# Attention and a gated feed-forward block on one core: stores of newly made weight parts stand four products later in the second pass

## The chip, the core and the metric

The kernel runs on one core of a Trainium2 chip. A core has several engines that run side by side, each through its own list of instructions in order: TensorE multiplies matrices (PE in the profile, its weight loads PEld), VectorE (DVE), ScalarE (ACT) and GpSimd (POOL) work element by element, and SyncE (SP) issues the transfers (DMAs) between the chip's large memory and the core's own memory. An engine that needs another's result waits for a semaphore, and everything behind the waiting instruction in its list waits too. The metric is the time of one execution in device microseconds; smaller is better.

## The reference: what is computed

Attention over 8 batches and 8 heads, 576 queries of 64 numbers each; keys and values are first averaged in groups of 8, so there are 72 of them. Its result, put together over the heads, is x, 4608 tokens of 512 numbers. A gated block follows:

```python
scores = scale * np.matmul(q, k_p.transpose(0, 1, 3, 2))   # k_p, v_p: means of 8
attn = softmax(scores)
x = (attn @ v_p) as 4608 x 512
gate = 1.0 / (1.0 + np.exp(-(x @ w_gate)))                 # w_gate: 512 x 1536
val = x @ w_val                                            # w_val:  512 x 1536
return (gate * val @ w_out)                                # w_out: 1536 x 512
```

## The kernel before

**Precision.** An operand of the feed-forward products is held as two parts, a high one and the rest, and a product is three matmuls (high by high, high by rest, rest by high). `split` (L165) makes the parts: a cast on ScalarE (L167), a subtraction on VectorE (L168).

**Seven products.** A 2 by 2 block product is made of seven smaller ones, m = 1 to 7 (`product`, L621 for its matmuls), instead of eight. For this the weights' quarters are added up: m = 1, 2, 3 take plain quarters of the weight, m = 4 to 7 sums of quarters. A product's result goes into a bank of TensorE's output memory; m = 1, 5 and 6 are copied out by ScalarE (L627, names sG1, sV5 and so on), m = 2, 3 and 7 are added to such a copy on VectorE (y, L633), then the gate side takes a sigmoid on ScalarE (L639) and the value side a multiplication by it on VectorE (h, L642). A bank can be filled again only when these have read it.

**Passes.** The tokens are cut in 12 blocks of 384, and a pass makes two of them: six passes. The weights of w_gate (G) and w_val (V) are cut in six pairs of columns, 0 to 5. In a pass, `hidden` goes through the pairs in the order `TURNS`, and for each pair through the 14 products of `SLOTS`, G and V mixed; then `second_sums` makes the second matmul (L834). Attention for the next pass's tokens runs as `tasks` between the products (scores L454, e L503, the exponential L508, attention times values L463).

**Weight parts.** Parts in use stand in a ring of eight buffers, `wpool`, tile name `parts`. The parts of a pair and kind are grouped as A (m = 1, 5), B (2, 6), C (3, 7) and D (4, 8; 8 is not used). A buffer holds one group, and after the group's last product it is loaded with the same group of the next pair (`loaded`, `reload`). In the text "G2C" is group C of gate pair 2.

**The second pass** is where the sums for pairs 0 to 4 are first made. The first pass has stored the plain parts (`kept...`) and the whole weights (`keptw...`) in the large memory. `prepare` loads a whole pair (512 KB, L254, tile w) and makes the four sums on VectorE (L255 to L257). `reload` with `fresh` then loads the group's plain part (256 KB, L297), splits the sum into the buffer's other half (L167, L168), and stores the new part (256 KB, `keep`, L213), so that later passes load both halves ready made. From the third pass on no part is made, but for pair 5, whose sums (`sums`, tile name sums) are made and stored early in the third pass.

**What sets the order.** The first pass is written out by hand (`ORDER`). From the second pass on a scheduler places each engine's instructions by times of its own, with the program's order as a start; an instruction passed to `tc.keep_in_program_order` keeps its place behind the last one before it on its engine. All transfers are issued on SP's one queue, in order: a store whose part isn't split yet holds every transfer behind it. SP also waits, at a transfer, for the one issued eight before.

Of the kernel before, what the change touches and what calls it, by code (L numbers as in the profile page):

```python
# [11 lines left out]
F32 = mybir.dt.float32  # L12
# [34 lines left out]
GROUPS = {"A": (1, 5), "B": (2, 6), "C": (3, 7), "D": (4, 8)}  # L47
# [77 lines left out]
def attention_then_ffn(ctx: ExitStack, tc: tile.TileContext, qT, kT, vm, vr, vn, sums8, wgv, wo, const, out, outT):  # L125
    nc = tc.nc
# [38 lines left out]
    def split(h, l, x):  # L165

        in_turn(nc.scalar.copy(h, x))  # L167
        in_turn(nc.vector.tensor_tensor(out=l, in0=x, in1=h.bitcast(F32), op=ALU.subtract))  # L168
# [3 lines left out]
    kept = {  # L172
        (kind, p, g): dram.tile([P, 2, 2 * HALF], F32R, name=f"kept{kind}{p}{g}")
        for p in range(NP) for kind in "GV" for g in GROUPS
    }
# [31 lines left out]
    def place(m):  # L207
        g = next(g for g, ms in GROUPS.items() if m in ms)
        return g, GROUPS[g].index(m)

    def keep(kind, p, m, t):
        g, i = place(m)
        nc.sync.dma_start(kept[kind, p, g][:, i].bitcast(F32), t.rearrange("p h n -> p (h n)").bitcast(F32))  # L213
# [52 lines left out]
    def sums(kind, p):  # L266

        if (kind, p) not in summing:
            fetch_for_sums(kind, p)
        w = summing.pop((kind, p))  # L270
        s = opool.tile([P, 4, HALF], F32, name="s4", tag="oparts")
        in_turn(nc.vector.tensor_tensor(out=s[:, 0:2], in0=w[:, 1:3], in1=w[:, 0:2], op=ALU.subtract))
        nc.vector.tensor_tensor(out=s[:, 2], in0=w[:, 2], in1=s[:, 0], op=ALU.subtract)
        nc.vector.tensor_tensor(out=s[:, 3], in0=w[:, 3], in1=s[:, 2], op=ALU.subtract)
        for i, ms in enumerate(((5, 7), (6, 4))):
            t = opool.tile([P, 2, 2, HALF], F32R, name="sums", tag="oparts")
            split(t[:, :, 0], t[:, :, 1], s[:, 2 * i:2 * i + 2])
            for k, m in enumerate(ms):
                keep(kind, p, m, t[:, k])
# [5 lines left out]
    def prepare(kind, p):  # L285
        summed[kind, p] = add_up(kind, p)

    def reload(kind, p, g, fresh=False):

        t = wpool.tile([P, 2, 2, HALF], F32R, name="parts", tag="parts")  # L290
        n = sum(m != 8 for m in GROUPS[g])
        for i, m in enumerate(GROUPS[g][:n]):
            parts[kind, p, m] = t[:, i]
        i = n - 1
        k = i if fresh else n
        if k:
            nc.sync.dma_start(  # L297
                t[:, :k].rearrange("p m h n -> p m (h n)").bitcast(F32), kept[kind, p, g][:, :k].bitcast(F32)
            )
        if fresh:  # L300
            split(t[:, i, 0], t[:, i, 1], summed[kind, p][:, SUM[g]])
            keep(kind, p, GROUPS[g][i], t[:, i])

    raws_o = {}

# [306 lines left out]
    def product(kind, p, m, stays=False):  # L612

        b = {1: "A", 6: "A", 7: "A", 4: "A", 2: "B", 5: "C", 3: "C"}[m]
        if m in (1, 2, 5):
            bank[kind, b] = ps.tile([P, BT], F32, name="chain", tag=CHAIN["GV".index(kind) * 3 + "ABC".index(b)])
        t, w, x = bank[kind, b], parts[kind, p, m] if stays else parts.pop((kind, p, m)), xo[m]
        for c in range(NC // 2):
            a = slice(c * P, (c + 1) * P)
            for k, (h, y) in enumerate(((0, 0), (0, 1), (1, 0))):  # L620
                nc.tensor.matmul(  # L621
                    t, lhsT=w[:, h, a], rhs=x[:, y, c],
                    start=(m in (1, 2, 5) and c == 0 and k == 0), stop=(c == 1 and k == 2), skip_group_check=True,
                )
        if m in (1, 5, 6):
            s = snap.tile([P, BT], F32, name=f"s{kind}{m}")
            nc.scalar.copy(s, t)  # L627
            seen[kind, m] = s
            return
        q = {2: (0, 0), 3: (0, 1), 7: (1, 1), 4: (1, 0)}[m]  # L630
        if m != 4:
            y = two.tile([P, BT], F32, name="y", tag="y")
            nc.vector.tensor_tensor(out=y, in0=t, in1=seen[kind, {2: 1, 3: 6, 7: 5}[m]], op=ALU.add)  # L633
        else:
            y = t
        if kind == "G":
            if m in (2, 7):
                gates[q[0]] = snap.tile([P, 2, BT], F32, name=f"gate{q[0]}")
            nc.scalar.activation(gates[q[0]][:, q[1]], y, AF.Sigmoid)  # L639
        else:  # L640
            f = 2 * p + q[1]
            nc.vector.tensor_tensor(  # L642
                out=hb[f // 4][:, f % 4, q[0] * BT:(q[0] + 1) * BT], in0=y, in1=gates[q[0]][:, q[1]], op=ALU.mult
            )

    def new_h(*ks):
        for k in ks or range(3):
            hb[k] = hpool.tile([P, NF // 3, 2 * BT], F32, name="h", tag=f"h{k}")
# [58 lines left out]
    def hidden(last, tasks, n):  # L707
        if n > 1:
            new_h()
        left = {}  # L710
        pairs = TURNS[n]
        for p, pair in enumerate(pairs):
            for i, (kind, m) in enumerate(SLOTS):
                if n == 1 and i == 3 and p + 1 < EARLY:
                    prepare("V", pairs[p + 1])
                if n == 1 and i == 10 and p + 2 < EARLY:
                    prepare("G", pairs[p + 2])
                if m < 0:
                    if p == 0:
                        continue  # L720
                    at, m = p - 1, -m
                else:
                    at = p
                stays = at + 1 == len(pairs) and not last
                product(kind, pairs[at], m, stays)
                if at + 1 < len(pairs):
                    loaded(kind, pairs[at], m, left, pairs[at + 1], n == 1)
                if n == 1 and i in (1, 4, 7, 10, 13) or n > 1 and (i % 3 == 2 or p == 0):
                    next(tasks, None)
                if n == 1:  # L730
                    if (p, i) in ((2, 4), (4, 4)):
                        first_sums(qs[1][p // 4])
                    if (p, i) in ((4, 7), (4, 11)):
                        operand(1, qs[1][i == 11], 1)
                    continue
                if p in (2, 4) and i == 4:
                    first_sums(qs[n][p // 2 - 1])
                if (p, i) in ((4, 10), (5, 6)):
                    operand(1, qs[n][p - 4], n)
                if n == 2 and (p, i) in ((1, 1), (2, 1)):  # L740
                    sums(*left_over.pop(0))
        for _ in tasks:
            pass

    def loaded(kind, p, m, left, then, fresh):

        g, i = place(m)
        left[kind, p, g] = left.get((kind, p, g), 0) + 1
        if left[kind, p, g] == sum(m != 8 for m in GROUPS[g]):
            reload(kind, then, g, fresh)  # L750
# [17 lines left out]
    def first_sums(q):  # L768

        at = len(s1)  # L770
        if at == 0:
            s1[None] = big.tile([P, 2, 2, BT], F32, name="s1", tag="big")
            at = 1
        s1[q] = s1[None][:, at - 1] if at < 3 else snap.tile([P, 2, BT], F32, name="s1", tag="gate0")
        minus(s1[q], quarter(q, 1, 0), quarter(q, 1, 1), ALU.add)
        if at < 3:
            third_sums(q)
# [9 lines left out]
    def operand(m, q, n):  # L787

        if m == 6:
            minus(s1[q], s1[q], quarter(q, 0, 0))  # L790
        if m == 3:
            minus(s1[q], quarter(q, 0, 1), s1[q])
        if m == 7 and q == qs[n][2]:
            third_sums(q)
        x = s1[q] if m in (5, 6, 3) else quarter(q, *{1: (0, 0), 2: (0, 1), 7: (1, 0), 4: (1, 1)}[m])
        hs = big.tile([P, 2, 2, BT], F32R, name="hs", tag="big")
        nc.scalar.copy(hs[:, 0], x)  # L797
        nc.vector.tensor_tensor(out=hs[:, 1], in0=x, in1=hs[:, 0].bitcast(F32), op=ALU.subtract)  # L798
        halves[m, q] = hs
# [387 lines left out]
    for n in range(NB // 2):  # L1187
        last = 2 * n + 2 == NB
        tasks, later = ahead[n:n + 2]
        steady[0] = n > 1  # L1190
        if n == 0:
            continue
        if n == 1:
            hidden_second(tasks)
        else:
            hidden(last, tasks, n)
        if last:
            build = iter(())
        else:
            build = operands()  # L1200
        if n < 1:
            second(tasks, build)
        else:
            second_sums(n, last, build, later)
# [46 lines left out]
```

## Time and profile before

| | |
|---|---|
| median of 3 runs | 975.35 us (972.98 to 976.16) |
| profiled execution | 973.47 us, span 971.7 us, mean granted clock of TensorE 0.993 |
| PE busy | 939.0 us, 97% of the span |
| DVE / ACT / POOL busy | 706.8 (73%) / 557.5 (57%) / 47.5 (5%) us |
| SP's transfer queue | 242.26 MB, 75.1% of 16 engines' span |
| chain that ended last | PE 71%, DVE 15%, DMA 7%, ACT 4%, issue 2% |

The span is the time from the first to the last instruction; 1.8 us of the execution lie around it. The chain that ended last is the row of work, followed back from the last instruction, that had nothing to spare. With PE busy for 97%, the kernel's length is PE's work plus the few stretches in which PE had to wait.

### The profile page before, as it was taken

To read this page: it belongs to the slowest core of one execution; us is meant where nothing else is said; L and a number is where in the kernel's file an instruction comes from. 1 tells how busy PE (TensorE), PEld (TensorE's weight loads), DVE (VectorE), ACT (ScalarE), POOL (GpSimd) and SP (SyncE) were. 2 spreads that over 40 slices of the span, in tenths; PEclk is the share of its full clock that TensorE was granted. 3 is DMA by queue.
4 is the path that set the end of the run, shared out by engine and by line. 5 is a ranking of instruction groups with operands and counts; after the bars stand their busy time and mean duration, and the time that the engine had idled before them with its cause. 6 is when DMAs were issued, how large, how long until landed. Compare 5 with 4: busy or idle time off the path is not lost.

```text
span 971.7 us, 15360 instructions
## 1 busy us (share of the span) xinstructions
PE 939.0 (97%) x5400; PEld 907.2 (93%) x5400; DVE 706.8 (73%) x1231; ACT 557.5 (57%) x1142; POOL 47.5 (5%) x67
## 2 busy tenths in 40 slices
PE   5899999999998999999999999999999999999998
PEld 4689998889998999999999999989999999999998
DVE  7999998787888878767796566599366578244474
ACT  6898966554666656645664555556355555233342
POOL 1210000000000000000000000000000000000000
PEclk8899999999999999999999999999999999999999
DMA  9978987769877377997479878567876637877566
GB/s 317 343 264 311 315 305 219 257 229 352 296 269 245 131 241 247 351 362 247 129 230 277 264 239 275 177 184 255 271 257 221 211 120 227 283 247 251 163 205 228
DMA packets 109883, 243.22 MB, mean 250 GB/s; under 512 B 11376, under 2 KB 45936, under 8 KB 108272
## 3 DMA queue, kind: packets, MB, share of 16 engines
q1 hardware_dynamic: 109808, 242.26, 75.1%
q8 instruction: 43, 0.70, 0.3%
q14 instruction: 32, 0.26, 0.1%
HBM read 191.88 MB, written 50.33 MB: 249 GB/s over the span
## 4 chain that ended last, share of the span: by engine, by line
PE 71%; DVE 15%; DMA 7%; ACT 4%; issue 2%; SPq 0%; DVEq 0%; ACTq 0%
PE chain L621 38%; PE acc L834 18%; PE chain L661 5%; PE acc L1147 3%; PE sc L454 3%; PE av L463 2%; DVE s L766 2%; DVE hs L798 1%; DMA out<-o 1%; DMA raw<-in_wgv 1%; DVE raw L197 1%; DVE w L199 1%; PE tp L542 1%; DVE zs L975 1%; DMA parts<-keptG1A 1%
## 5 line engine op out<-in xcount | busy, mean ns | idle before, releaser
L621 PE MATMUL chain<-xo,parts 128*128 128x384 f32 x2436 | 457.5, 341 | 7.6 <-ACT sG L627 2.5
L621 PEld LDWEIGHTS chain<-xo,parts 128*128 128x128 f32 x2436 | 424.0, 188 | 12.1 <-ACT sG L627 3.7
L834 PE MATMUL acc<-hs,oparts 128*128 128x384 f32 x1260 | 229.2, 336 | 3.2 <-DVE hs L798 2.8
L834 PEld LDWEIGHTS acc<-hs,oparts 128*128 128x128 f32 x1260 | 218.2, 188 | 6.0 <-DVE hs L798 4.4
L633 DVE TENSOR_TENSOR y<-chain,sG 128x384 f32<-128x384 f32 x87 | 47.8, 552 | 79.1 <-ACT sG L627 27.6
L661 PE MATMUL chain<-xo,parts 128*128 128x384 f32 x504 | 93.7, 340 | 0.8 <-ACT xs L1086 0.8
L661 PEld LDWEIGHTS chain<-xo,parts 128*128 128x128 f32 x504 | 87.9, 188 | 2.6 <-ACT xs L1086 1.1
L627 ACT COPY sG<-chain 128x384 f32<-128x384 f32 x87 | 41.5, 477 | 55.5 <-PE chain L621 55.1
L633 DVE TENSOR_TENSOR y<-chain,sV 128x384 f32<-128x384 f32 x87 | 47.5, 550 | 35.1 <-PE chain L621 26.4
L798 DVE TENSOR_TENSOR hs<-h,hs 128x768 fp32r<-128x768 f32 x60 | 58.1, 973 | 17.1 <-ACT hs L797 17.1
L627 ACT COPY sV<-chain 128x384 f32<-128x384 f32 x87 | 41.3, 476 | 50.0 <-PE chain L621 45.5
L639 ACT ACTIVATE gate<-y 128x384 f32<-128x384 f32 x87 | 45.5, 525 | 41.2 <-DVE y L633 40.7
L797 ACT CAST hs<-h 128x768 fp32r<-128x768 f32 x60 | 49.9, 834 | 25.4 <-PE acc L834 25.1
L536 POOL TENSOR_TENSOR pm<-e,rz 128x384 f32<-128x384 f32 x32 | 29.2, 912 | 610.7 <-DVE rz L516 224.7
L797 ACT CAST hs<-s 128x768 fp32r<-128x768 f32 x45 | 37.0, 835 | 34.4 <-PE acc L834 22.7
L1147 PE MATMUL acc<-oparts,hs 128*128 128x512 f32 x216 | 51.7, 392 | 0.4 <-DVE hs L1137 0.4
L642 DVE TENSOR_TENSOR h<-y,gate 128x384 f32<-128x384 f32 x87 | 49.0, 567 | 1.8
L798 DVE TENSOR_TENSOR hs<-s,hs 128x768 fp32r<-128x768 f32 x45 | 42.5, 954 | 8.3 <-ACT hs L797 8.0
L1147 PEld LDWEIGHTS acc<-oparts,hs 128*128 128x128 f32 x216 | 40.2, 188 | 8.7 <-DVE hs L1137 0.8
L454 PE MATMUL sc<-kbd,raw 128*128 128x144 f32 (+1 forms) x280 | 47.6, 308 | 0.0
L454 PEld LDWEIGHTS sc<-kbd,raw 128*128 128x128 f32 (+1 forms) x280 | 38.3, 187 | 6.6 <-issue 4.0
L546 DVE TENSOR_TENSOR pl<-tp,ph 128x384 fp32r<-128x384 f32 x32 | 17.6, 551 | 26.7 <-ACT ph L545 26.7
(186 smaller groups left out, 1182.0 us busy)
## 6 DMA issues: line engine op xcount, KB each, us to landing
oparts<-keptS SPq DMA_DIRECT2D x60, 512.0 KB, 4.4
oparts<-keptO SPq DMA_DIRECT2D x90, 256.0 KB, 3.8
raw<-in_wgv SPq DMA_DIRECT2D x12, 1024.0 KB, 6.7
raw<-in_qT SPq DMA_DIRECT2D x42, 192.0 KB, 4.3
out<-o SPq DMA_DIRECT2D x40, 192.0 KB, 4.3
raw<-in_kT SPq DMA_DIRECT2D x26, 288.0 KB, 4.1
raw<-in_vm SPq DMA_DIRECT2D x28, 256.0 KB, 4.1
raw_o<-in_wo SPq DMA_DIRECT2D x12, 512.0 KB, 4.4
```

Source lines behind the costliest of these rows:

```text
L454: nc.tensor.matmul(sc[lo - i * P:hi - i * P, i], lhsT=q[:, lo:hi], rhs=kbd[slot(b, p)], start=True, stop=True)
L536: nc.gpsimd.tensor_tensor(out=pm, in0=e[:, n, :, :KM], in1=rz[:, n, :, None].broadcast_to([P, 2 * QT, KM]), op=ALU.mult)
L621: nc.tensor.matmul(t, lhsT=w[:, h, a], rhs=x[:, y, c], start=(m in (1, 2, 5) and c == 0 and k == 0), stop=(c == 1 and k == 2), skip_group_ ...
L627: nc.scalar.copy(s, t)
L633: nc.vector.tensor_tensor(out=y, in0=t, in1=seen[kind, {2: 1, 3: 6, 7: 5}[m]], op=ALU.add)
L639: nc.scalar.activation(gates[q[0]][:, q[1]], y, AF.Sigmoid)
L642: nc.vector.tensor_tensor(out=hb[f // 4][:, f % 4, q[0] * BT:(q[0] + 1) * BT], in0=y, in1=gates[q[0]][:, q[1]], op=ALU.mult)
L661: nc.tensor.matmul(t, lhsT=w[:, c // 2, h, a], rhs=x[:, y, c % 2], start=(c == 0 and k == 0), stop=(c == NC - 1 and k == 2),)
L797: nc.scalar.copy(hs[:, 0], x)
L798: nc.vector.tensor_tensor(out=hs[:, 1], in0=x, in1=hs[:, 0].bitcast(F32), op=ALU.subtract)
L834: nc.tensor.matmul(acc[name, c], lhsT=w[:, k, h, c * P:(c + 1) * P], rhs=hs[:, y, k], start=(m in (1, 2, 5) and i % 3 == 0 and k == 0 and ...
L1147: nc.tensor.matmul(acc[i], lhsT=hss[f][:, y, a], rhs=oparts[f][:, w], start=(f == 0 and k == 0), stop=(f == NF - 1 and k == 2),)
```

## The change

`reload` no longer issues the store of a new part. It puts it on a list, `due`, with a count of 4. `keep_due`, called after each product of `hidden`, takes one from each count and issues the stores whose count is used up; it is also called at the head of every `reload`, for stores of the same kind and group (an older pair's) alone, and at the end of the pass for all that are left. Each of these stores is passed to `keep_in_program_order`, so that it stays behind the SP instruction traced just before it. Nothing is computed otherwise, and the same transfers are made.

```diff
     def reload(kind, p, g, fresh=False):
 
+        keep_due(room=(kind, g))
         t = wpool.tile([P, 2, 2, HALF], F32R, name="parts", tag="parts")
...
         if fresh:
             split(t[:, i, 0], t[:, i, 1], summed[kind, p][:, SUM[g]])
-            keep(kind, p, GROUPS[g][i], t[:, i])
+            due.append([LATER, kind, p, GROUPS[g][i], t[:, i]])
+
+
+    LATER = 4
+    due = []
+
+    def keep_due(all=False, room=None):
+        for d in due:
+            d[0] -= room is None
+        for d in [d for d in due if all or d[0] <= 0 or (d[1], place(d[3])[0]) == room]:
+            due.remove(d)
+            _, kind, p, m, t = d
+            g, i = place(m)
+            tc.keep_in_program_order(
+                nc.sync.dma_start(kept[kind, p, g][:, i].bitcast(F32), t.rearrange("p h n -> p (h n)").bitcast(F32))
+            )
...
                 if at + 1 < len(pairs):
                     loaded(kind, pairs[at], m, left, pairs[at + 1], n == 1)
+                keep_due()
...
         for _ in tasks:
             pass
+        keep_due(True)
```

Since the scheduler places the other instructions around these stores, all engines but POOL get another order, from about 230 us to about 554 us of the trace before. Three places follow. Lines of the kernel after are 1 higher for `reload`'s load (L298), L317 for the moved store, and 16 higher from there on (L642 becomes L658).

First SP, the transfers around the parts of pair 2, before. The names are those above; a store is `kept... <- parts`, a load `parts <- kept...`, and w8 is a whole weight loaded for its sums.

```order
L297 DMA parts_3203<-keptG2B_143 128x512
L380 DMA raw_4208<-in_qT 128x384
L213 DMA keptV1D_141<-parts_3175 128x512
L254 DMA w8_3289<-keptwG3_180 128x1024
L213 DMA keptG2B_143<-parts_3203 128x512
L297 DMA parts_3241<-keptG2C_144 128x512
L213 DMA keptG2C_144<-parts_3241 128x512
L297 DMA parts_3273<-keptV2A_146 128x512
L213 DMA keptV2A_146<-parts_3273 128x512
L213 DMA keptG2D_145<-parts_3285 128x512
L297 DMA parts_3317<-keptV2B_147 128x512
L254 DMA w8_3408<-keptwV3_181 128x1024
```

The same place on SP after:

```order
L298 DMA parts_3201<-keptG2B_143 128x512
L317 DMA keptG2A_142<-parts_3152 128x512
L254 DMA w8_3287<-keptwG3_180 128x1024
L298 DMA parts_3240<-keptG2C_144 128x512
L317 DMA keptG2B_143<-parts_3201 128x512
L298 DMA parts_3272<-keptV2A_146 128x512
L317 DMA keptG2C_144<-parts_3240 128x512
L298 DMA parts_3315<-keptV2B_147 128x512
L317 DMA keptV2A_146<-parts_3272 128x512
L317 DMA keptG2D_145<-parts_3283 128x512
L254 DMA w8_3406<-keptwV3_181 128x1024
```

The load of G2C now stands ahead of the store of G2B, and the load of V2B ahead of the store of G2D; the load of the whole V3 still stands behind the store of G2D.

Next DVE, a little later, before: L255 is the first sum of the whole V3 and waits for its load.

```order
L642 TENSOR_TENSOR h_2381<-y_3337,gate1_3239 128x384
L255 TENSOR_TENSOR w8_3408<-w8_3408 128x512
L633 TENSOR_TENSOR y_3428<-chain_3421,sG1_3374 128x384
L256 TENSOR_TENSOR w8_3408<-w8_3408 128x256
L168 TENSOR_TENSOR parts_3385<-w8_3289,parts_3385 128x256
L418 TENSOR_TENSOR vl0_101<-vs_3125,vh0_96 64x64 x2
L257 TENSOR_TENSOR w8_3408<-w8_3408 128x256
L500 TENSOR_REDUCE m_3261<-sc_3257 128x6
L642 TENSOR_TENSOR h_2381<-chain_3246,gate1_3239 128x384
L503 TENSOR_TENSOR e_3208<-sc_3257,m_3261 128x432
```

The same place on DVE after:

```order
L519 TENSOR_TENSOR e_3206<-sc_3256,m_3260 128x432
L649 TENSOR_TENSOR y_3336<-chain_3244,sV5_3270 128x384
L649 TENSOR_TENSOR y_3426<-chain_3419,sG1_3372 128x384
L255 TENSOR_TENSOR w8_3406<-w8_3406 128x512
L168 TENSOR_TENSOR parts_3384<-w8_3287,parts_3384 128x256
L658 TENSOR_TENSOR h_2381<-y_3336,gate1_3238 128x384
L529 TENSOR_REDUCE zs_3207<-e_3206 128x12
L256 TENSOR_TENSOR w8_3406<-w8_3406 128x256
L413 TENSOR_REDUCE ks_4210<-raw_4211 128x72
L168 TENSOR_TENSOR parts_3402<-w8_3177,parts_3402 128x256
L649 TENSOR_TENSOR y_3451<-chain_3375,sG6_3417 128x384
L562 TENSOR_TENSOR pl_3120<-tp_3115,ph_3119 128x384
```

e and a y have moved ahead of L255. The last h of V1, which reads the chain's bank (chain_3246 before, chain_3244 after), stood eight rows behind L255 (the doubled row counts as two) and is eleven behind it now: three rows follow the last one shown, a small zs, L257 and then this h.

Last ACT, where the copy sG6 of G2 is made, before:

```order
L639 ACTIVATE gate0_3430<-y_3428 128x384
L167 CAST parts_3404<-w8_3179 128x256
L508 ACT_TABLE_LOAD
L508 ACTIVATE e_3208<-e_3208 128x864
L797 CAST hs_3688<-h_2383 128x768
L627 COPY sG6_3419<-chain_3367 128x384
```

The same place on ACT after:

```order
L524 ACT_TABLE_LOAD
L524 ACTIVATE e_3206<-e_3206 128x864
L643 COPY sV5_3492<-chain_3485 128x384
L655 ACT_TABLE_LOAD
L655 ACTIVATE gate0_3428<-y_3426 128x384
L167 CAST parts_3402<-w8_3177 128x256
L643 COPY sG6_3417<-chain_3365 128x384
```

The sigmoid of the gate has moved behind the exponential, and with it a second load of a function table stands ahead of sG6.

## Rows read from the trace of the kernel before

**Rows 1.** Windows by stretch: ends, length, busy us of PE, PEld, DVE, ACT, POOL (instructions), clock, DMA share, GB/s.

```profile
226.00:288.00 62.00, 61.89 (x375) 59.88 (x373) 51.34 (x118) 39.18 (x93) 2.86 (x3) 1.00 0.91 310
288.00:306.00 18.00, 13.98 (x86) 13.18 (x85) 14.06 (x28) 9.33 (x22) 1.20 (x1) 1.00 0.70 235
306.00:554.00 248.00, 247.42 (x1465) 243.19 (x1465) 191.23 (x330) 147.81 (x285) 12.97 (x14) 1.00 0.75 248
554.00:971.70 417.70, 408.38 (x2367) 400.56 (x2365) 255.85 (x425) 200.24 (x379) 12.17 (x14) 1.00 0.69 225
```

**Rows 2.** What PE waited for, 226 to 306 us: total us, times, longest.

```profile
PE chain L621 <- ACT sG L627: 1.9, 1, 1.9
PE chain L621 <- DMA parts<-keptG2C: 1.2, 1, 1.2
PE chain L621 <- DVE h L642: 1.0, 1, 1.0
```

**Rows 3.** What SP's queue waited for, 226 to 306 us: total us, times, longest.

```profile
SPq L213 <- DVE parts L168: 13.5, 9, 4.9
```

**Rows 4.** SP's timeline: start, length, queue, line, transfer.

```profile
282.04 0.42 SPq L254 DMA_DIRECT2D w<-keptwG  x1
282.55 0.39 SPq L213 DMA_DIRECT2D keptG2B<-parts  x1
283.03 0.39 SPq L297 DMA_DIRECT2D parts<-keptG2C  x1
...
290.57 0.32 SPq L213 DMA_DIRECT2D keptG2D<-parts  x1
...
291.79 0.46 SPq L254 DMA_DIRECT2D w<-keptwV  x1
```

**Rows 5.** DVE's timeline; in brackets the idle time before and its releaser.

```profile
288.09 0.69 DVE L255 TENSOR_TENSOR w<-w 128x512 f32<-128x512 f32 x1 [2.71 <-DMA w<-keptwG]
...
290.13 0.42 DVE L168 TENSOR_TENSOR parts<-w,parts 128x256 fp32r<-128x256 f32 x1
...
297.40 0.69 DVE L255 TENSOR_TENSOR w<-w 128x512 f32<-128x512 f32 x1 [3.22 <-DMA w<-keptwV]
...
300.50 0.55 DVE L642 TENSOR_TENSOR h<-chain,gate 128x384 f32<-128x384 f32 x1
300.97 0.60 DVE L503 TENSOR_TENSOR e<-sc,m 128x432 f32<-128x432 f32 x1
```

**Rows 6.** ACT's timeline.

```profile
301.64 1.28 ACT L508 ACT_TABLE_LOAD   x1 [2.22 <-DVE e L503]
302.94 0.92 ACT L508 ACTIVATE e<-e 128x864 f32<-128x864 f32 x1
...
304.49 0.47 ACT L627 COPY sG<-chain 128x384 f32<-128x384 f32 x1
```

**Rows 7.** PE's timeline.

```profile
289.48 4.46 PE L621 MATMUL chain<-xo,parts 128*128 128x384 f32 x24 [1.18 <-DMA parts<-keptG2C]
...
294.64 0.92 PE L454 MATMUL sc<-kbd,raw 128*128 128x144 f32 x6
```

**Rows 8.** Loads of parts by line L297, 226 to 321 us: issue to landing.

```profile
DMA to landing us min/median/max: 2.7/4.4/6.5
```

**Rows 9.** SP's and PE's timeline in the third pass.

```profile
382.27 0.40 SPq L264 DMA_DIRECT2D w<-keptwV  x1
...
394.34 0.37 SPq L213 DMA_DIRECT2D keptV5A<-sums  x1
...
398.40 0.92 SPq L297 DMA_DIRECT2D parts<-keptV2C  x1
...
401.78 5.48 PE L621 MATMUL chain<-xo,parts 128*128 128x384 f32 x30
```

**Rows 10.** SP's and PE's timeline at the start of the second pass's products.

```profile
246.00 0.45 SPq L297 DMA_DIRECT2D parts<-keptG0C  x1
...
254.38 4.09 PE L621 MATMUL chain<-xo,parts 128*128 128x384 f32 x22
```

## The prediction

> **What bounds the kernel now.** I read the windows by stretch first. The length of a stretch less PE's busy time is what PE lost there. The products of the second pass up to 288 us lose 0.11 us of 62.00; the 18 us from 288 to 306 lose 4.02; the rest of the second pass with the third loses 0.58 in 248; the last four passes lose 9.32 in 417.7, the kernel's tail included [rows 1]. So PE's work is the bound, and only its gaps can be won. The order changes from about 230 to 554 us alone, so the change can at most win the gaps there, 0.11 + 4.02 + 0.58 = 4.71 us, nearly all of them in 18 us.
>
> The list of PE's waits names them: G2C's load 1.2 us, a copy sG 1.9 us, an h 1.0 us [rows 2], 4.1 together, rounded, against those 4.02 us. What is behind each is read from SP's and DVE's timelines. The load of G2C goes out at 283.03, right behind the store of G2B and the load of the whole G3 [rows 4], and PE starts with it at 289.48, 6.45 us later [rows 7]. The other two have one cause. The store of G2D goes out at 290.57 [rows 4], when its split (290.13 + 0.42) is done [rows 5]; the load of the whole V3 stands behind it and goes out at 291.79 [rows 4] (SP's longest wait for a split there is 4.9 us [rows 3]); DVE sits 3.22 us at L255 until it lands at 297.40, and h (300.50) and e (300.97) stand behind [rows 5]. e releases the table load, the exponential follows, and sG6 only then, at 304.49 [rows 6].
>
> **The change, part by part.** It removes no transfer and no arithmetic; 40 stores of 256 KB (five pairs, two kinds, four groups) are put off. On PE, DVE and SP as many instructions stand as before; ACT has one pair of table loads more, 2 x 1.28 us [rows 6] on an engine that is busy 9.33 us of the 18 [rows 1]; it counts only through sG6, below.
>
> *G2C.* Its load now stands ahead of G2B's store and behind the load of the whole G3 as before. What it no longer waits for is DVE's split of G2B and 256 KB of bytes. It was late by 1.2 us [rows 2]. Loads of this line land in 2.7 to 6.5 us, median 4.4, this one in the slowest way [rows 8]; at the median it would be early by 0.9 us. Bounds: 0 (it lands as slowly, the whole G3 being still ahead) and -1.2. I take -1.2: the row that it is nearest to is the median.
>
> This is the place at which a rule bears. The row shows a load behind a store taking 6.45 us [rows 4, 7] where the median is 4.4 [rows 8]. The Trainium skill, page "DMA: Bandwidth & Descriptors", section "Queues, rings and completion order", says that a transfer's completion mark on a DMA engine lands only after every earlier write of that engine, whichever transfer it belonged to. By that rule a late bunch of stores slows each load behind it, and the gain at G2C is given back at the next load that stands behind one, so that the sum would be that of the third rival below, 978.5 for 974.1. That rival is worked out from rows alone, and the traces show this one slow load, not a rule.
>
> *The wait at L255.* The store of G2D still stands ahead of the load of the whole V3, and its split now stands as the seventh DVE instruction from L255 of G3 where it was the fourth. One DVE instruction in the stretch takes 14.06 / 28 = 0.50 us [rows 1]. V2B's load no longer stands between them. The split comes three such instructions, 1.5 us, later, and the whole G3 itself goes out earlier, as only one store stands between it and G2B's load, where a store and another load stood; I estimate 0.7 us. That makes V3's load go out at about 291.2 for 291.79. With the 5.6 us that it took (291.79 to 297.40 [rows 4, 5]) L255 runs at 296.8.
> What is new is what stands behind it. e now runs ahead of L255: sixteen instructions from L255 of G3 (at 288.09 before [rows 5], so at about 287.4 now), so it ends near 287.4 + 16 x 0.50 = 295.4 for 301.57. ACT then makes a table load 1.28, exponential 0.92, sV5 0.47, a second table load 1.28, a sigmoid 0.5, a split 0.4 and sG6 0.47 (sV5 taken as sG6, sigmoid and split as their nearest rows on DVE, 0.55 and 0.42) [rows 5, 6]. It pipelines a little, so sG6 is done near 300.6, for 304.96.
> PE without the wait for G2C would be at 288.3 (289.48 less 1.18 [rows 7]). A product is six matmuls; four take 4.46 us, 1.1 each; the eight attention matmuls 0.7 (from 293.94 to 294.64) and a set of scores 0.9 at most. Up to G2's m = 7 it has eight products, eight attention matmuls and two sets of scores: 8.8 + 0.7 + 1.8 = 11.3, so 299.6. It waits 1.0 for sG6, where it waited 1.9.
> h of V1 is eleven behind L255, 296.8 + 11 x 0.50 = 302.3, or up to 303.5 if the split right behind L255 is held by its buffer. PE wants it after G2's m = 7, G3's m = 5 and eight more attention matmuls: 300.6 + 2.2 + 0.7 = 303.5. So the wait of 1.0 goes, or keeps some 0.2. Then, however, the y that G2's m = 4 needs stands six instructions behind that h, at 305.3 to 306.5 and 0.55 long; PE is there two products later, at 305.9. That is 0 to 1.2 us late, and I take 0.8.
> Sum here: 1.0 + 0.2 + 0.8 = 2.0 for 2.9 before, -0.9. Bounds: -2.9 (nothing waits) and +1.5 (the sigmoid's table load and the buffer both come out late).
>
> *The third pass.* It loses 0.58 in 248 us, the four that follow it 9.32 in 417.7 [rows 1], about 1.5 to 2.3 each with the tail out or in. The third now gets another order, with the stores of pair 5's sums between loads. It can win the 0.58 and can lose what other passes lose more, 1.7. I take +0.6, nearer to its own row than to the others'.
>
> *The start.* Seven stores now go out in a row ahead of G0C's load, which went out at 246.00 and is used by the second product of the row at 254.38, so at 255.5 [rows 10]. It has 9.5 us, and needs 4.4 at the median, 6.5 at most [rows 8]: 3 to 5 us of cover. Seven issues at 0.3 to 0.5 us are 3.0 us (0.32 to 0.46 each [rows 4]). I take +0.2, bounds 0 and +1.5.
>
> Sum: -1.2 - 0.9 + 0.6 + 0.2 = -1.3 us. The profiled execution was 973.47 (span 971.7 and 1.8 around it), so 972.2; the median shown stands 1.88 above that execution, so **974.1** against 975.35. 0.3% is 2.9 us, about what a measurement here can tell from no change, so the likeliest finding is no change.
>
> **The rivals.**
> *All three gaps close.* For it: they have one common cause, stores ahead of loads, and the change takes just that away. Against: V3's load still stands behind G2D's store, and e, h and y are reshuffled on DVE, not freed. Then -1.2 - 2.9 - 0.4 of the third pass = -4.5: 970.9.
> *Hidden anyway, or not done.* The scheduler may order so that the loads leave when they did; the loads wait for PE to free a buffer before anything else. For it: two of three gaps hang on G2D's split, which isn't earlier. Against: the order shows G2C's load moved. Then the gaps move and stay: 975.4.
> *A store that holds a load in the third pass (slower).* The load of the whole V5 went out at 382.27, V5A's store of the sums made from it at 394.34, 12.1 us later; V2C's load at 398.40 [rows 9]. In the order after, V5's load stands behind G2B's load and G5's last stores, some five transfers later, near 387, so V5A's store near 399, and V2C's load now stands right behind that store. PE wants V2C as the fourth product of the row at 401.78, at 405.0 [rows 9]. It lands 2.7 to 6.5 us after issue [rows 8], so it decides from an issue at 405.0 - 4.4 = 400.6 on: at 399.4 the price is 0 to 0.9; if the store waits for DVE once more as long as the longest did here, 4.9 us [rows 3], the load goes out at 404.3 and the price is 3.7. With a smaller gain in the second pass, -0.6 + 3.7 = +3.1: 978.5.
>
> **How the numbers follow.** Forecast with its own spread (972.4 to 976.4): 0.56. All gaps close: 0.23. Hidden or not done: 0.08. The slower case: 0.13. The first rival mostly passes the 2.9 us bound, and the forecast's lower edge adds a little: faster 0.25. Slower: 0.13. Same: 0.62. The range takes in the first rival's larger part and the slower one's beginning: 971.0 to 977.6.
>
> **What the profile after would show.** PE's waits without G2C's load: right in the first step; with that load still named, wrong. DVE's wait for the whole V3 at L255 shorter than 3.22 us, by 1 or more, with e ahead of it: right in the second; a wait of PE for sG6 of about 1 us and for y at G2's m = 4. Windows: 288 to 306 losing 2 to 3 us, the third pass 1 to 1.5. The prediction is wrong if the second pass loses under 1 us, or if the third loses over 3.

## The result: slower by 0.3%, and the profile after

The kernel after takes 977.18 us (median of 20 runs, 974.53 to 982.29) against 973.94 (20 runs, 971.88 to 977.54) for the kernel before: ratio 1.0032, 95% interval 1.0021 to 1.0043. That is 3.1 us slower, where 1.3 us faster was forecast. Its profiled execution has a span of 976.4 us.

The windows of the kernel after, with the columns of [rows 1]:

```profile
226.00:288.00 62.00, 61.57 (x373) 59.65 (x372) 51.23 (x116) 39.23 (x93) 3.33 (x4) 1.00 0.90 308
288.00:306.00 18.00, 17.79 (x110) 16.97 (x109) 16.59 (x36) 13.07 (x29) 0.99 (x1) 1.00 0.82 256
306.00:554.00 248.00, 242.00 (x1417) 235.07 (x1417) 184.70 (x315) 142.01 (x273) 12.44 (x13) 1.00 0.73 241
```

The 18 us that lost 4.02 now lose 0.21: in this execution the gaps that the change was aimed at are gone. The 248 us that lost 0.58 now lose 6.00. PE's waits from 226 to 306 us (total, times, longest):

```profile
PE chain L637 <- DVE y L649: 0.4, 1, 0.4
PE chain L637 <- DMA parts<-keptG2C: 0.2, 1, 0.2
```

and from 306 to 560 us:

```profile
PE chain L637 <- DMA parts<-keptG3C: 2.0, 1, 2.0
PE acc L852 <- ACT hs L815: 1.9, 2, 1.2
PE acc L852 <- DVE hs L816: 1.0, 2, 0.7
PE chain L637 <- DVE y L649: 0.5, 2, 0.3
PE tp L539 <- DVE r L492: 0.4, 1, 0.4
```

Against [rows 2], G2C's wait has fallen from 1.2 to 0.2, and those for sG (1.9) and h (1.0) are no longer there. G2C's load landed no earlier, though: at 289.37 us, for 289.35 in the kernel before. It is PE that came to it later, at 289.20 for 288.30. New are G3C's load (2.0) and waits for hs, the operand of the second matmul (L852), whose high part ACT casts and whose rest DVE makes: once in the second pass (1.2, at 330 us) and three times in the third. The timeline of PE there:

```profile
497.89 0.62 PE L852 MATMUL acc<-hs,oparts 128*128 128x384 f32 x2 [0.67 <-ACT hs L815]
498.41 1.00 PE L470 MATMUL sc<-kbd,raw 128*128 128x144 f32 x6
499.16 0.61 PE L852 MATMUL acc<-hs,oparts 128*128 128x384 f32 x2
500.14 6.51 PE L852 MATMUL acc<-hs,oparts 128*128 128x384 f32 x36 [0.38 <-DVE hs L816]
...
508.12 8.09 PE L852 MATMUL acc<-hs,oparts 128*128 128x384 f32 x45 [0.67 <-DVE hs L816]
```

and of DVE and ACT just ahead of it:

```profile
493.77 0.95 DVE L168 TENSOR_TENSOR xo<-xs,xo 128x768 fp32r<-128x768 f32 x1
494.63 0.60 DVE L516 TENSOR_REDUCE m<-sc 128x6 f32<-128x432 f32 x1
495.15 0.95 DVE L784 TENSOR_TENSOR s<-s,h 128x768 f32<-128x768 f32 x1
496.02 0.95 DVE L784 TENSOR_TENSOR s<-h 128x768 f32<-128x768 f32 x1
...
497.00 2.30 ACT L815 CAST hs<-s 128x768 fp32r<-128x768 f32 x3 [3.17 <-DVE s L784]
```

ACT sits idle for 3.17 us until DVE has made the sum s, and DVE makes it only after a split of the next pass's operand (xo) and a maximum of attention scores. In the kernel before the two sums stand at 490.99 and 491.87 us, and PE waits 0.2 us in all for an hs between 480 and 530 us:

```profile
490.99 0.96 DVE L766 TENSOR_TENSOR s<-s,h 128x768 f32<-128x768 f32 x1
491.87 0.95 DVE L766 TENSOR_TENSOR s<-h 128x768 f32<-128x768 f32 x1
...
494.35 9.43 PE L834 MATMUL acc<-hs,oparts 128*128 128x384 f32 x53
```

No part of w_gate or w_val is on the way near this place: from 478 to 512 us SP issues loads of w_out's parts and of attention's inputs alone, and the last store that the change moves (V3D, at 322.11) went out 170 us earlier.

### The profile page after: what moved, and what is told of

It reads as the page before. It is cut to its first block, busy times and chain, and to the rows that moved or that the text cites. A ratio compares the mean times of both kernels' runs of the same rounds, so it can differ in the third digit from the quotient of the medians.

```text
span 976.4 us, 15353 instructions
## 1 busy us (share of the span) xinstructions
PE 940.9 (96%) x5400; PEld 907.8 (93%) x5400; DVE 707.3 (72%) x1231; ACT 559.6 (57%) x1144; POOL 46.7 (5%) x67
## 4 chain that ended last, share of the span: by engine, by line
PE 69%; DVE 15%; DMA 9%; ACT 4%; issue 2%; SPq 1%; DVEq 0%; ACTq 0%
PE chain L637 37%; PE acc L852 18%; PE chain L677 5%; PE acc L1165 3%; PE sc L470 3%; PE av L479 2%; DVE s L784 1%; DVE hs L816 1%; DMA out<-o 1%; DMA raw<-in_wgv 1%; DVE raw L197 1%; PE tp L558 1%; DMA parts<-keptG3C 1%; DVE w L199 1%; DVE zs L993 1%
## 5 line engine op out<-in xcount | busy, mean ns | idle before, releaser
L852 PE MATMUL acc<-hs,oparts 128*128 128x384 f32 x1260 | 228.7, 336 | 6.3 <-DVE hs L816 3.7
L852 PEld LDWEIGHTS acc<-hs,oparts 128*128 128x128 f32 x1260 | 218.4, 188 | 10.0 <-DVE hs L816 5.5
L658 DVE TENSOR_TENSOR h<-y,gate 128x384 f32<-128x384 f32 x87 | 48.0, 555 | 1.9
```

The costliest lines, as they stand in the source:

```text
L658: nc.vector.tensor_tensor(out=hb[f // 4][:, f % 4, q[0] * BT:(q[0] + 1) * BT], in0=y, in1=gates[q[0]][:, q[1]], op=ALU.mult)
L852: nc.tensor.matmul(acc[name, c], lhsT=w[:, k, h, c * P:(c + 1) * P], rhs=hs[:, y, k], start=(m in (1, 2, 5) and i % 3 == 0 and k == 0 and ...
```

## The experiments

Two theories. **A**: the stores' later place is harmless or good, and the loss comes from the other order into which the scheduler puts everything else once these stores stand elsewhere. **B**: stores put off come in bunches and hold loads or buffers further on.

Most experiments need one order changed and the rest held. A list per engine is added to the kernel, and after the kernel is traced each instruction is tied behind the one ahead of it in the list, so that the scheduler has no choice left from the second pass on (no run ties the order of before with nothing moved):

```diff
+    for engine, text in QUEUES.items():
+        queue = [traced[engine][k] for k in order_of(text)]
+        for a, b in zip(queue, queue[1:]):
+            tc.add_manual_dep(b, a.name, mybir.DependencyInfo(mybir.DependencyClass.NoSync, ...), reason="order")
...
         attention_then_ffn(tc, *aps, o, oT)
+        in_this_order(tc)
```

The list is read off the kernel before, off the kernel after, or pieced together of both. Below, a shift between two traces is the difference of the start of the same matmul, at a point where PE has done the same work in both. Ratios are against the kernel before, run on the same chip beside them.

### Which pass loses the time

Third pass as before, second pass as after:

```diff
 QUEUES: what starts before 383 us in the trace of before: in the order of the kernel after
         the rest:                                         in the order of the kernel before
```

> All engines are tied: what starts before 383 us in the trace of before (the second pass) in the order of the kernel after, the rest in the order before. From the traces, the second pass of after loses what it gains (G2C, h and sG gone, 4.1 us; G3C 2.0, hs 1.2, small y waits come). Theory A: -0.5 to +1.5 us on before, since the third pass carries most of the loss. Theory B (the loss comes in the pass in which the stores are put off): +2.5 to +4 us, as in the kernel after.

Measured: 974.38 us against 974.93, ratio 0.9987 (0.9973 to 1.0002). The second pass in its new order, with all its stores put off, costs nothing. From 220 to 400 us the trace gains 0.5 us (shift +0.27, then -0.21). It had gained more on the way: the shift is -2.9 at 305 us and back at -0.7 by 371. PE's waits from 226 to 306 us, and from 306 to 400:

```profile
PE chain L790 <- DMA parts<-keptG2C: 1.2, 1, 1.2
...
PE acc L1003 <- ACT hs L966: 1.2, 1, 1.2
PE chain L790 <- DVE y L802: 0.4, 1, 0.4
PE chain L790 <- ACT sV L796: 0.2, 1, 0.2
```

The waits for h and sG are gone, as in the kernel after. The one for G2C is as long as before, against the expectation: the load stands ahead of G2B's store here too, and landed at 289.62.

The other way round, with no store of a new part put off:

```diff
 QUEUES: what starts before 383 us in the trace of before: in the order of the kernel before
         the rest:                                         in the order of the kernel after
```

> All engines are tied: what starts before 383 us in the trace of before in the order before, with the stores at once; the rest (the third pass) in the order of the kernel after. No store of a new part is put off here. Theory A: +2 to +3.5 us on before, with PE waiting for hs near 495 to 508 us. Theory B: within 1 us of before.

Measured: 979.77 against 974.93, ratio 1.0043 (1.0027 to 1.0059). The shift is +0.19 us at 400, +1.1 at 494 and +3.5 at 560. Up to 400 us, where this run is tied in the order of before, the shift stays between +0.1 and +0.4, so the ties themselves cost nothing there. The third pass's order alone makes the whole loss. Narrowed down, with 480 us for 383:

> All engines are tied: what starts before 480 us in the trace of before in the order before, the rest (from the third pass's second matmul on) in the order of the kernel after. Theory A, with its place: DVE takes the next pass's attention work (an xo split, a maximum, sums of x, e) ahead of the sums that hs is cast from, PE waits for hs: +2 to +3 us on before, lost between 494 and 512 us. Rival: the loss came with the third pass's weight products, whose loads stand among the stores of pair 5's sums: within 1 us of before.

Measured: 979.01 against 975.76, ratio 1.0042 (1.0026 to 1.0059). The shift goes from +3.2 us at 480 to +4.3 at 494 and +6.6 at 514 (the +3.2 was there before the order differs, and is this execution's own). PE's waits between 480 and 530 us:

```profile
PE acc L1003 <- DVE hs L967: 1.1, 2, 0.7
PE acc L1003 <- ACT hs L966: 0.7, 1, 0.7
PE tp L711 <- ACT xs L722: 0.7, 1, 0.7
```

The three waits for hs are those of the kernel after, to a tenth; the one for xs, ahead of them, the kernel after doesn't have. So the order from the third pass's second matmul on is enough for a loss of the same size. From 494 to 514 us, where the waits for hs stand, the shift grows by 2.3 us, and by as much in the kernel after (+2.2 to +4.5) and with the whole third pass new; these two lose some 0.9 us more between 403 and 494.

A look at the cause, in the order of the kernel after:

```diff
 DVE, third pass, second matmul:
-m<-sc   s<-s,h   s<-h   s<-xs   e<-sc,m   h<-h   hs<-s
+s<-s,h   s<-h   m<-sc   e<-sc,m   h<-h   hs<-s   s<-xs
```

> All engines are tied in the order of the kernel after, and two DVE instructions of the third pass's second matmul move: a maximum of attention scores (0.52 us) behind the two sums s that hs is cast from, and the first sum of x (0.87 us) behind the hs that follows. Theory A's mechanism (attention work ahead of the sums makes hs late): PE's wait for the cast hs near 498 us (0.67 us) falls to 0.2 or less and the wait for DVE's hs near 500 us (0.38 us) goes. Rival (ACT or PE's own order makes hs late): both waits stay.

Measured, one profile: ACT's wait falls as theory A has it, DVE's does not.

```profile
494.78 0.62 PE L1004 MATMUL acc<-hs,oparts 128*128 128x384 f32 x2 [0.16 <-ACT hs L967]
...
496.88 7.13 PE L1004 MATMUL acc<-hs,oparts 128*128 128x384 f32 x36 [0.38 <-DVE hs L968]
```

0.67 has become 0.16: the maximum ahead of the sums was 0.5 of the 0.67. The rest hs is still waited for by 0.38, so that half of the expectation was wrong: between the sums and this rest the maximum, e and h now stand, where the sum of x, e and h stood. Nor is any time won. The 36 matmuls behind this wait take 7.13 us where the kernel after has them in 6.51, the third wait is again 0.67, and from 494 to 514 us the shift grows by 2.5 us, for 2.3 in the kernel after. DVE is busy for all 18 us from 494 to 512 in the kernel after, so what is moved back on it may hold what follows. That DVE's order sets the first of these waits is shown; which instructions' places make the loss is not.

The one execution's time (981.05) has no interval. Its SP order is that of the kernel after, and there PE waited 0.2 us for G3C, not 2.0; with the second pass alone new, no wait for G3C is listed. That wait comes and goes from run to run, and isn't in the 3.1 us as a whole.

### Whether late stores cost something themselves

In the lists of SP below, w(G3) is the load of the whole G3 and q a load of queries.

```diff
 SP: 25 of 40 stores, each:
-load  store(its new part)  load  load
+load  load  load  store
```

> Every engine's instructions are tied in the order of the kernel before; only 25 of the 40 stores of new parts stand later on SP, each behind the loads of parts and whole weights that stand ahead of it in the kernel after. Theory A (the later stores are good, the loss comes from the new order of everything else): G2C's wait of 1.2 us goes, the waits for h and sG may shrink, nothing else moves: 0.5 to 3 us faster than before. Theory B (stores put off come in bunches and hold later loads): 1 to 4 us slower than before, with a wait of PE for a load of parts of 1 us or more between 290 and 320 us.

Measured: 977.19 against 974.93, ratio 1.0023 (1.0007 to 1.0039). The time is in theory B's range, so stores put off can cost something themselves, but the wait isn't the one that B named. The shift comes in one step of 1.8 us between 240 and 260 us, at a cast on ACT and the copy behind it:

```profile
250.10 0.40 ACT L336 CAST parts<-w 128x256 fp32r<-128x256 f32 x1 [1.75 <-DMA keptV4A<-parts]
```

and PE's wait for it, from the list of waits (total, times, longest):

```profile
PE chain L790 <- ACT sV L796: 1.4, 1, 1.4
```

The cast refills a buffer whose old part (V4A) isn't stored yet; V4A's store went out at 246.57, second of a row of seven (246.09 to 250.40). With that row undone:

```diff
 SP: as above, but the stores up to V0A's at once behind their loads
```

> As the first experiment (order of before, stores of new parts later), but the stores up to V0A's stand at once behind their loads as before, so that no seven of them go out in a row at the start. In the first experiment PE waited 1.4 us at 251 us for a copy sV behind a cast that waited for V4A's store. Theory A: that wait goes, and 1.5 to 2 us with it: 1 us faster than before to 0.5 slower. Theory B: the later stores hold other casts in the same way: still 1.5 us or more slower than before.

Measured: 976.33 against 975.21, ratio 1.0013 (0.9999 to 1.0027). The step at 250 us is gone, yet nothing is won: sG (1.8 us) is still waited for, for the whole V3 still stands behind G2D's store. The time lies between the two ranges expected, and its interval reaches no change. In the kernel after the same cast waits 1.8 us for the same store, but nothing in its own order needs that part at once: PE waits for no sV there, only 0.4 us for a y.

PE, DVE, ACT and POOL in the order of after, SP in the order of before:

```diff
 QUEUES: PE, DVE, Activation, Pool: after;  SP: before
```

> PE, DVE, ACT and POOL are tied in the order of the kernel after; SP is tied in the order of the kernel before, with each store at once behind its load, as before. Theory A: slow like the kernel after, +2 to +5 us on before, with PE's waits for hs at the two second matmuls. Theory B: the bunches are gone, so within 1 us of before or faster.

Measured: 1001.42 against 974.93, ratio 1.0267. The two orders don't fit (PE waits 5.9 us for a load of queries alone), so this tells nothing of the theories.

### Does the loss follow the count?

```diff
-    LATER = 4
+    LATER = 8        # and 2 in the second run
```

> The kernel after with the count 8 for 4. Theory A: the scheduler makes yet another order; the time is anywhere from -3 to +6 us on before and does not follow the count, with the loss or gain mostly outside the second pass's products. Theory B: stores put off twice as far hold buffers and loads more: slower than the kernel after, +5 us or more on before, lost in the second pass.

> The kernel after with the count 2 for 4. Theory A: another order again, -3 to +6 us on before. Theory B: half as far, so between before and the kernel after: +1 to +2 us.

Measured: 8 gives 977.65 (ratio 1.0030, 1.0016 to 1.0044), 2 gives 980.23 (1.0053, 1.0033 to 1.0074). Theory B expected 5 us or more and 1 to 2 us; both intervals exclude that. Least put off has the slowest median, so the loss doesn't follow the count. The waits are other ones each time. PE's largest with 8, from 226 us on:

```profile
PE chain L637 <- ACT gate L655: 2.2, 1, 2.2
PE chain L637 <- ACT sG L643: 1.4, 1, 1.4
```

and with 2:

```profile
PE chain L637 <- DVE y L649: 1.7, 2, 1.3
PE chain L637 <- ACT sG L643: 1.5, 2, 0.8
PE av L479 <- DVE pl L562: 1.3, 1, 1.3
```

Part of theory A's expectation failed: 8 lost 1.8 us in the second pass's products (shift +0.39 at 240, +2.21 at 280, back to +0.48 at 316) and more in its second matmul, not outside it.

### Only the stores that held something

```diff
 SP, order of before:
-w(G3)  store G2B  load G2C  ...  store G2D  load V2B  w(V3)  load V2C
+w(G3)  load G2C  store G2B  ...  load V2B  w(V3)  load V2C  store G2D
```

> All engines are tied in the order of the kernel before; on SP only two of the 40 stores move: G2B's store right behind G2C's load, and G2D's store behind the loads of V2B, the whole V3 and V2C. Theory A (a store waiting for its split held those loads, and the new order of everything else cost the time): G2C's load leaves about 0.5 us earlier, the whole V3's about 2 us, so PE's waits for G2C, h and sG shrink from 4.1 us to under 1.5: 2.5 to 4 us faster than before. Theory B (a store put off costs as much further on): within 1 us of before or slower, with a wait of PE for another load of parts or another split.

Measured: 972.39 against 975.21, ratio 0.9978 (0.9961 to 0.9994), 2.1 us faster. SP, DVE and PE there:

```profile
281.86 0.42 SPq L466 DMA_DIRECT2D parts<-keptG2C  x1
...
290.57 0.32 SPq L423 DMA_DIRECT2D w<-keptwV  x1
...
292.11 0.42 SPq L382 DMA_DIRECT2D keptG2D<-parts  x1
...
294.10 0.69 DVE L424 TENSOR_TENSOR w<-w 128x512 f32<-128x512 f32 x1
...
289.35 4.46 PE L790 MATMUL chain<-xo,parts 128*128 128x384 f32 x24 [1.68 <-DMA parts<-keptG2C]
```

The whole V3 goes out 1.2 us earlier than in [rows 4] and lands before DVE asks for it: L255's sum (L424 here) waits 3.22 us no more [rows 5], and the waits for h and sG are gone. G2C's load goes out 1.17 us earlier and lands no earlier (289.22 for 289.35). So its delay was not the store's wait for a split. Next, with G2D's store moved as above, its load goes further ahead:

```diff
-load G2B  q  store V1D  w(G3)  load G2C  store G2B
+load G2B  q  load G2C  store V1D  w(G3)  store G2B
```

> As the experiment with two stores moved, and G2C's load stands ahead of V1D's store and of the load of the whole G3 as well. There G2C's load left 1.2 us earlier than in the kernel before (281.86 for 283.03) and landed no earlier (289.22 for 289.35), so it seems held by what was issued ahead of it. Theory A1 (768 KB ahead of it held it): it lands 1.5 us or more earlier, PE's wait of 1.7 us for it goes, 3.5 to 5 us faster than before. Theory A2 (it is held by all that moves at that time, ahead or behind): the wait stays at 1 us or more, 2.5 to 3 us faster than before, as with two stores moved.

Measured: 972.71 against 975.76, ratio 0.9964 (0.9950 to 0.9979): 3.5 us faster than before. The wait for G2C is gone (theory A1), though the load goes out a microsecond later (282.90) than with two stores moved: it landed at 286.13, 3.23 us after its issue, where it took 7.36 there. So it was held by the 768 KB that stood ahead of it. Whether the store or the load among these held it wasn't tried apart. The trace of the kernel after speaks for the load: there V1D's store had landed at 283.84, just after G2C's load went out (283.70), and G2C's load still took 5.67 us and landed 0.64 behind the whole G3 (288.73). What comes up in its place is the sum of G3's weights, now behind it, and a y on DVE behind that:

```profile
PE chain L790 <- DVE y L802: 1.0, 1, 1.0
PE chain L790 <- ACT sG L796: 0.5, 1, 0.5
```

By its ratio this is the fastest kernel here, though its interval overlaps that of two stores moved: it moves two stores and one load, and holds every other instruction where it was.

## Why the prediction was wrong

*What bounds the kernel* held: PE, with 4 us of gaps in 18 us.

*G2C, -1.2.* It came to -1.0 in the profile after, by luck. This step failed too: the load went out at 283.70, later than before (283.03), and landed at 289.37 for 289.35; PE's own lateness of 0.9 us hid the rest of the wait. With only the second pass new, the wait is 1.2 as before. The load was not late for the split or the store of G2B. The reason that the prediction gave for its bound of 0, the whole G3 ahead of the load, fits the runs better.

*The wait at L255, -0.9.* L255 ran at 296.99 (296.8 worked out), again by luck: the whole G3 went out at 283.18, not 0.7 us ahead of 282.04, and the whole V3 at 292.30, not 291.2, but it took 4.67 us and not 5.6. DVE waited 0.56 us there, e stood at 294.90 and sG6 was done at 300.68 (300.6). PE reached the product behind sG6 at 300.73, where 299.6 had been worked out. So PE's waits for sG and h went from 2.9 to nothing that is listed, where 1.2 were left in the sum; the y of G2's m = 4 kept 0.3 of 0.8. The term is mis-sized, on the good side.

*The third pass, +0.6: the step that failed.* It was sized as a draw between the 0.58 that was lost from 306 to 554 us and what later passes lose, and it was taken near its own row: 1 to 1.5 us in all. Measured are 6.00, where the prediction named 3 as the sign of being wrong. The row holds the end of the second pass as well, for which the sum has no term of its own: up to 340 us G3C (2.0), hs (1.2) and a y (0.3) are waited for there. And the later passes were divided wrongly: of six passes three are left, not four, so they lose 3.1 us each with the tail in, and the bound of this term was 2.5, not 1.7. The third pass's order alone costs about 4 us (ratio 1.0043 with nothing else changed), more than that bound too. A stretch that loses 0.58 us in 248 had little to win by any reordering, and much to lose. The order was to be had before the run, and showed DVE's split and maximum ahead of the sums, but only its SP part was read for this pass.

*The start, +0.2.* 0.3 in the profile (a loss of 0.43 in the first window for 0.11, a y), within its bounds.

*The slower rival* had the right sign and pass, and the wrong place: it put the loss on V2C's load behind V5A's store. PE never waited for V2C. PE's waits are for hs, from ACT and DVE, in the second matmul, where no moved transfer is near. The slow-load rule of the Trainium skill (page "DMA: Bandwidth & Descriptors", section "Queues, rings and completion order") was given that rival's price. Where the loss stands PE waits for no load, so the rule isn't its cause here. At G2C's load, which landed 0.6 us behind the whole G3 with G2B's store moved behind it, no run separates the rule from the bytes.

So more than the expected gain was made in those 18 us: 3.8 in the profile. About 1.3 are left at the end of the second pass (ratio 0.9987, whose interval reaches no change; an hs at 330 us, and G3C in the profiled run, take from it), and 4.1 are lost from there on (1.0043; 1.0042 with only the order from 480 us on new): 2.8 together, against the 3.1 measured. The time of 977.18 lies within the range named, 971.0 to 977.6, but that range reached so far up for a rival that didn't happen.

## What to carry to other kernels

Where a scheduler places the instructions, moving 40 transfers is a new order for all engines: read what it does to the stretches that lose nothing now, and price those as the thing at risk. If a gap hangs on a few transfers, move these and tie the rest down: two stores gave 2.1 us, two stores and a load 3.5, where moving all gave -3.1. A load's lateness can come from what stands ahead of it, not from when it is issued: look at when it lands, not only at how long it is waited for, since a wait also shrinks when PE comes late. And a wait that gets shorter is a gain only if the time behind it does too.

## What was not expected of the hardware

A 256 KB load issued 1.17 us earlier (281.86 for 283.03) landed at 289.22 for 289.35, after 7.36 us for 6.32, and one issued at 282.90 ahead of 768 KB landed at 286.13, after 3.23 us. A 512 KB load (the whole V3, issued at 290.57) landed at 293.93, after 3.36 us, where the one of [rows 4, 5] took 5.6.
